# Packed attention and two MLP blocks on one core: the attention and weight steps of the next batch set beside other units

## The chip, the core and the metric

One core of a Trainium2 chip runs the whole program in one launch. The metric is device time in microseconds, the median of several runs. Three runs of the kernel before took 1697.84, 1701.42 and 1705.88 us, so runs of one kernel lie up to 0.5% apart.

## What is computed

Three stages in a row, all in float32 results:

```python
# 8 batches, 8 heads, 576 tokens, head size 64; 32 packed queries
p_packed = sm_attn(p, k, v)                  # 32 x 576 scores per head
out      = sm_attn(q, p_packed, p_packed)    # 576 x 32 scores per head
x = out.transpose(0, 2, 1, 3).reshape(4608, 512)
x = moe(x)    # h = x @ w_in (512 x 2048); (h * sigmoid(1.702 h)) @ w_out
y = moe2(x)   # g = x @ w_gate (512 x 1536); (silu(g) * (x @ w_val)) @ w_out2
```

The weights come as 64-bit floats and are turned into 32-bit ones on the chip. A float32 product is made as three products of a high and a low part (`split` makes the two parts, `mm3` issues the three matmuls).

## The kernel before

**Units.** The first MLP runs as 256 units: 8 batches, 2 halves of 288 tokens, 16 slices of 128 hidden columns. Unit n issues `u_p1(n)` (6 matmuls into a PSUM tile `h`), `act2` of unit n-1 (a copy on ScalarE, a subtraction on VectorE), `u_act1(n)` (tanh on ScalarE, a product `g` on VectorE, which frees `h`; there are two `h` tiles) and `p2` of unit n-3 (12 matmuls into the accumulators `acc`). A batch is 32 units, numbered u = 0 to 31 below. The second MLP follows after the last unit and is not touched.

**Steps beside the units.** While batch b goes through its units, the attention of batch b+1 is computed in small steps, and the weights of the second MLP are converted, six tiles of 128x512 in each of six batches. Which steps follow which unit is written out in two tables of text: `SECOND` has the steps of batch 1's attention beside the units n = 19 to 33 (the last 13 units of batch 0, and units 0 and 1 of batch 1), `STEADY` has those beside u = 0 to 31 of batches 1 to 6. Batch 0 and the first steps of batch 1's attention are in a third table, `FIRST`, and batch 7 has code of its own. The main loop issues the unit, then SECOND's steps, then STEADY's:

```python
        p2(units[n - LAG])
        if n in SECOND:
            issue(SECOND[n], ops, second)
        if 0 < b < B - 1 and u in STEADY:
            issue(STEADY[u], ops)
```

The program is laid out by a scheduler that takes this order as the order of preference: an instruction whose buffer is not yet free, or whose input is not ready by the scheduler's own reckoning, is put behind later ones of its engine. Once laid out, each engine, and SyncE as the queue that issues nearly all DMAs, goes through its instructions strictly in order.

**The steps, in the order in which a batch needs them** (g is one of two groups of four heads, j one of four raw tiles: K of g = 0, 1, then Q of g = 0, 1; e one of two halves):

- `raw_ahead n` loads a raw tile three ahead (four DMAs of 144 KB; three `raw` buffers, so each waits until `do_T` has read the tile that had the buffer); `v_ahead g` and `p_ahead` load V (five DMAs) and p of the batch after.
- `do_p`, `split_p`; `do_T j e` transposes a raw tile on VectorE (`T`, two buffers); `split_T j e` splits it (`Th`, two buffers), by ScalarE and GpSimd, or with `dve` by ScalarE and VectorE.
- `sc1 g` (12 matmuls), `max1`, `exp1`, `norm1`, `a1T` (5 transposes on TensorE), `copy_a1T`, `pv g` (20 matmuls): the first attention. `do_D g` copies its result out of PSUM in eight 32x32 copies on VectorE, or with `act` on ScalarE, and makes one masked copy on VectorE; `split_D`, `split_E` split both.
- `sc2 g t` (6 matmuls for one half t of the tokens), `max2`, `exp2`, `norm2` (five instructions on VectorE), `split_a2`: the second attention; the result `a2` is the moving operand of the next batch's `p1`.
- `win j` loads one of 16 tiles of the split `w_in` (512 KB) into a `wh` buffer, of which there are three. `do_z n` (n = 0 to 7) needs tiles 2n and 2n+1: four matmuls into two PSUM tiles `zp`, then copies, sums and a split on ScalarE, VectorE and GpSimd give `z`, the stationary operand of `p1`.
- `w2_stage i` loads a 64-bit weight tile into one of the same three `wh` buffers, `w2_rebias` and `w2_to_f32` convert it on ScalarE and VectorE, `w2_store` writes it back to DRAM.

All PSUM results of the attention (`sc`, `a1T`, `pv`, `zp`) share two buffers of one pool.

Of the kernel before, what the change touches and what calls it, by code (L numbers as in the profile page):

```python
# [53 lines left out]
"""  # L54

SECOND = {
# [15 lines left out]
}  # L72

STEADY = {
    0: "do_p; w2_stage 0",
    1: "split_p; p_ahead; do_T 0 0",
# [30 lines left out]
}  # L107


# [861 lines left out]
```

## Time and profile before

| | |
|---|---|
| time, median of 3 runs | 1701.42 us (1697.84 to 1705.88) |
| the profiled execution, time | 1701.6 us |
| its span | 1699.9 us |
| TensorE busy | 1633.9 us, 96% of the span |
| VectorE / ScalarE / GpSimd busy | 1208.0 (71%) / 773.8 (46%) / 291.6 us (17%) |
| mean granted TensorE clock | 0.994 of full speed |

Times inside the profile count from the start of the span, of which 1.7 us of the execution's own time lies outside. "PE" is TensorE, "DVE" VectorE, "ACT" ScalarE, "POOL" GpSimd, "SP" SyncE. A line such as L508 is a line of the kernel; L209 and L210 are the copy and the subtraction inside `split`, L220 the matmul inside `mm3`, L281 the DMA of `win`, L252 and L255 those of `load_raw` for K and Q, L339 the transpose of `do_T`, L508 and L511 the matmul and the sum of `do_z`, L558 the product of `u_act1`. In brackets stands the idle time of the engine before an instruction and what ended it.

### The profile page before, as it was taken

The page shows a single profiled execution, that of the slowest core. Times are in us where ns is not written, and L with a number is a line of the kernel's source. Part 1 is how long each engine was busy: PE and PEld are TensorE (multiplying, and loading weights), DVE is VectorE, ACT ScalarE, POOL GpSimd, SP SyncE. Part 2 cuts the span into 40 slices and gives each one's busy share as a digit, 9 for nine tenths or more (in the row PEclk, how much of TensorE's full clock was granted, in tenths as well). Part 3 has the DMA queues.
Part 4 walks back from the last instruction along what each step waited for, and adds up shares of the span by engine and source line. Part 5 has one row for each costly group of instructions (what it writes and reads, how often), then busy time and mean ns, then how long its engine had stood idle before and what let it go on. Part 6 is the DMA issues. An engine that isn't in the chain of part 4 may idle for free.

```text
span 1699.9 us, 25897 instructions
## 1 busy us (share of the span) xinstructions
PE 1633.9 (96%) x9264; PEld 1455.7 (86%) x9264; DVE 1208.0 (71%) x2284; ACT 773.8 (46%) x1606; POOL 291.6 (17%) x241
## 2 busy tenths in 40 slices
PE   5689999999999999999999999999999999999998
PEld 4569899999989999999988888888888888888887
DVE  6988988788777878868589366575567456756662
ACT  4775756657565665746455222242224222322222
POOL 1332403122121312202012110100010010001010
PEclk9989999999999999999999999999999999999999
DMA  8874856647364564616388554444444354425411
GB/s 232 297 240 108 255 163 209 199 161 240 119 203 143 202 206 142 225 41 221 109 288 324 206 178 153 149 130 155 143 160 155 95 175 163 149 77 171 151 50 50
DMA packets 169345, 290.60 MB, mean 171 GB/s; under 512 B 54784, under 2 KB 96768, under 8 KB 169216
## 3 DMA queue, kind: packets, MB, share of 16 engines
q1 hardware_dynamic: 165760, 280.03, 50.4%
q10 hardware_dynamic: 3456, 8.91, 1.5%
q8 instruction: 73, 1.20, 0.3%
q14 instruction: 56, 0.46, 0.1%
HBM read 230.16 MB, written 58.72 MB: 170 GB/s over the span
## 4 chain that ended last, share of the span: by engine, by line
PE 81%; DVE 8%; issue 4%; DMA 3%; ACT 2%; POOL 1%; SPq 0%; ACTq 0%; DVEq 0%; POOLq 0%
PE acc L220 34%; PE gv L220 29%; PE h L220 9%; PE sc L220 3%; PE pv L404 3%; PE zp L508 2%; DVE z L511 1%; DMA wh<-win 1%; DVE gh L210 1%; DVE g L558 1%; DVE f L205 1%; PE a1T L387 1%; DVE wc L203 0%; ACT z L510 0%; DMA w64in<-in_moe_w_in_dram 0%
## 5 line engine op out<-in xcount | busy, mean ns | idle before, releaser
L220 PE MATMUL gv<-xh,w 128*128 128x512 f32 x2304 | 554.4, 389 | 0.0
L220 PEld LDWEIGHTS gv<-xh,w 128*128 128x128 f32 x2304 | 432.4, 188 | 89.7
L220 PE MATMUL acc<-gh,wo 128*128 128x288 f32 x3072 | 457.8, 297 | 5.9 <-ACT wo L209 2.0
L220 PEld LDWEIGHTS acc<-gh,wo 128*128 128x128 f32 x3072 | 427.4, 190 | 10.3 <-ACT wo L209 2.9
L220 PE MATMUL acc<-wo,gh 128*128 128x512 f32 x1296 | 326.8, 389 | 0.4
L220 PEld LDWEIGHTS acc<-wo,gh 128*128 128x128 f32 x1296 | 243.0, 188 | 52.1 <-DVE c L214 1.7
L220 PE MATMUL h<-a,z 128*128 128x288 f32 x1536 | 253.6, 299 | 7.6 <-DVE g L558 6.0
L210 DVE TENSOR_TENSOR gh<-g,gh 128x288 fp32r<-128x288 f32 (+1 forms) x295 | 180.7, 612 | 89.1 <-ACT gh L209 87.3
L220 PEld LDWEIGHTS h<-a,z 128*128 128x128 f32 x1536 | 223.6, 191 | 18.0 <-DVE g L558 9.3
L209 ACT CAST gh<-g 128x288 fp32r<-128x288 f32 (+1 forms) x304 | 140.3, 461 | 176.9 <-DVE g L558 128.7
L210 POOL TENSOR_TENSOR gh<-s,gh 128x512 fp32r<-128x512 f32 x60 | 82.2, 1370 | 699.2 <-ACT gh L209 655.4
L802 DVE TENSOR_TENSOR c<-gv,c 128x512 f32<-128x512 f32 x192 | 132.1, 688 | 83.9 <-ACT tb L817 56.7
L209 ACT CAST gh<-s 128x512 fp32r<-128x512 f32 x60 | 37.3, 621 | 247.3 <-DVE s L813 229.5
L556 ACT ACTIVATE sig<-h 128x288 f32<-128x288 f32 x256 | 104.1, 408 | 86.9 <-PE h L220 82.5
L558 DVE SCALAR_TENSOR_TENSOR g<-sig,h 128x288 f32<-128x288 f32 x256 | 113.7, 444 | 33.7 <-ACT sig L556 30.9
L802 DVE TENSOR_TENSOR ta<-gv,c 128x512 f32<-128x512 f32 x96 | 66.1, 689 | 83.4 <-PE gv L220 83.4
L513 POOL TENSOR_TENSOR z<-z,z 128x512 fp32r<-128x512 f32 x56 | 75.0, 1339 | 170.9 <-ACT z L512 170.9
L511 DVE TENSOR_TENSOR z<-zp,z 64x512 f32<-64x512 f32 x112 | 77.0, 687 | 18.4 <-ACT z L510 15.3
L508 PE MATMUL zp<-wh,E 128*128 128x512 f32 x224 | 66.3, 404 | 12.6 <-DMA wh<-win 6.6
L822 ACT ACTIVATE s<-c 128x512 f32<-128x512 f32 x48 | 30.3, 632 | 95.9 <-DVE c L802 95.9
L510 ACT COPY z<-zp 64x512 f32<-64x512 f32 x112 | 65.0, 581 | 9.5 <-PE zp L508 7.0
L210 POOL TENSOR_TENSOR Th<-T,Th 128x576 fp32r<-128x576 f32 x30 | 44.2, 1483 | 125.2 <-ACT Th L209 125.2
(130 smaller groups left out, 1585.6 us busy)
## 6 DMA issues: line engine op xcount, KB each, us to landing
w<-w2s SPq DMA_DIRECT2D x144, 512.0 KB, 3.3
wh<-win SPq DMA_DIRECT2D x112, 512.0 KB, 4.2
w2s<-w SPq DMA_DIRECT2D x36, 512.0 KB, 3.8
w<-w2s SPq DMA_DIRECT2D x48, 256.0 KB, 2.6
raw<-in_k_dram SPq DMA_DIRECT2D x64, 144.0 KB, 3.9
raw<-in_q_dram SPq DMA_DIRECT2D x64, 144.0 KB, 4.0
x2d<-x SPq DMA_DIRECT2D x16, 576.0 KB, 3.8
w2d<-f SPq DMA_DIRECT2D x36, 256.0 KB, 3.2
```

The source lines that it names most:

```text
L209: ACT.copy(dst[:, 0], src)
L210: eng.tensor_tensor(out=dst[:, 1], in0=src, in1=dst[:, 0].bitcast(F32), op=ALU.subtract)
L220: PE.matmul(o, lhsT=lhs(a), rhs=rhs(c), start=first and n == 0, stop=last and n == 2)
L404: PE.matmul(ps[:, c].rearrange("p h i -> p (h i)"), lhsT=vv[:n, k, 2 * c:2 * c + 2].rearrange("p h d -> p (h d)"), rhs=st["a1T", g][:n, k, ...
L508: PE.matmul(ps, lhsT=E[:, c].rearrange("p a i -> p (a i)"), rhs=w[c][:, d], start=d == 0, stop=d == 1)
L510: ACT.copy(x[o], ps[r])
L511: DVE.tensor_tensor(out=x[o], in0=ps[o], in1=x[o], op=ALU.add)
L513: POOL.tensor_tensor(out=y[:, 1], in0=x, in1=y[:, 0].bitcast(F32), op=ALU.subtract)
L556: ACT.activation(s, ps[:, :HS], AF.Tanh, scale=0.5 * 1.702)
L558: DVE.scalar_tensor_tensor(out=g, in0=s, scalar=1.0, in1=ps[:, :HS], op0=ALU.add, op1=ALU.mult)
L802: DVE.tensor_tensor(out=o, in0=ps, in1=c, op=ALU.add)
L822: ACT.activation(s2, c2, AF.Tanh, scale=0.5)
```

## The change

Both tables are written anew. `FIRST`, the functions and the main loop stay as they are. The two tables hold the same steps as before, 71 and 113 of them, with these exceptions in their arguments: in `STEADY` `do_D 0` has `act`, `split_T 2 1` has `dve` and `split_T 3 1` has lost it; in `SECOND` `do_D 0` has `act` and `split_D 0` has `dve`. Everything else is a step at another unit, or at another place among the steps of its unit.

```diff
--- before.py
+++ after.py
@@ -54,56 +54,55 @@
 """
 
 SECOND = {
-    19: "+do_T 2 0; +max1 1; +exp1 1; +do_T 2 1; +win 0; +win 1; +win 2; +norm1 1",
-    20: "+a1T 0; +copy_a1T 0; +split_T 2 0 dve; +split_T 2 1; +raw_ahead 2",
-    21: "+pv 0; +do_D 0; +split_D 0; +split_E 0; +v_ahead 0; +a1T 1",
-    22: "+copy_a1T 1",
-    23: "+sc2 0 0; +max2 0 0; +pv 1; +do_D 1",
-    24: "+split_D 1; +split_E 1; +sc2 0 1; +max2 0 1; +do_T 3 0",
-    25: "+split_T 3 0 dve; +do_T 3 1; +do_z 0; +win 3; +win 4; +split_T 3 1 dve",
-    26: "+sc2 1 0; +raw_ahead 3; +max2 1 0; +do_z 1; +win 5; +win 6",
-    27: "+sc2 1 1; +v_ahead 1; +max2 1 1; +exp2 0 0; +do_z 2; +win 7; +win 8",
-    28: "+norm2 0 0; +exp2 1 0; +split_a2 0 0; +norm2 1 0; +exp2 0 1",
-    29: "+do_z 3; +win 9; +win 10; +split_a2 1 0; +norm2 0 1; +exp2 1 1",
-    30: "+split_a2 0 1; +norm2 1 1; +do_z 4; +win 11; +win 12; +split_a2 1 1",
-    31: "+do_z 5; +win 13; +win 14",
-    32: "+do_z 6; +win 15",
+    19: "+do_T 2 0; +split_T 2 0 dve; +win 1; +max1 1; +exp1 1; +win 4; +norm1 1; +raw_ahead 2; +do_T 2 1",
+    20: "+do_T 3 0; +win 0; +win 2; +a1T 0; +split_T 2 1",
+    21: "+copy_a1T 0; +pv 0; +win 3; +do_D 0 act; +split_D 0 dve; +raw_ahead 3",
+    22: "+a1T 1; +copy_a1T 1; +split_E 0; +do_T 3 1; +v_ahead 1",
+    23: "+sc2 0 0; +max2 0 0; +split_T 3 1 dve; +do_z 0; +pv 1; +do_D 1",
+    24: "+split_D 1; +split_E 1; +sc2 0 1; +exp2 0 0",
+    25: "+split_T 3 0 dve; +v_ahead 0",
+    26: "+sc2 1 0; +sc2 1 1; +do_z 1; +max2 0 1; +win 5; +win 6; +max2 1 0",
+    27: "+do_z 2; +win 7; +max2 1 1",
+    28: "+norm2 0 0; +win 8; +exp2 1 0; +split_a2 0 0; +norm2 1 0; +exp2 0 1; +win 13",
+    29: "+do_z 3; +split_a2 1 0; +norm2 0 1; +exp2 1 1; +win 9",
+    30: "+split_a2 0 1; +win 10; +norm2 1 1; +split_a2 1 1; +do_z 4; +win 11; +win 12",
+    31: "+do_z 5; +win 14",
+    32: "+win 15; +do_z 6",
     33: "+do_z 7",
 }
 
 STEADY = {
-    0: "do_p; w2_stage 0",
-    1: "split_p; p_ahead; do_T 0 0",
-    2: "w2_stage 1; do_T 0 1",
-    3: "w2_rebias 0; split_T 0 0; do_T 1 0; w2_to_f32 0",
-    4: "w2_stage 2; w2_store 0; split_T 0 1 dve; sc1 0; do_T 1 1",
-    5: "w2_rebias 1; max1 0; raw_ahead 0; w2_to_f32 1",
-    6: "exp1 0; w2_stage 3; w2_store 1; split_T 1 1; norm1 0",
-    7: "split_T 1 0; w2_rebias 2; w2_to_f32 2",
-    8: "raw_ahead 1; w2_stage 4; sc1 1; w2_store 2",
-    9: "do_T 2 0; w2_rebias 3; max1 1; exp1 1; w2_to_f32 3",
-    10: "do_T 2 1; w2_stage 5; w2_store 3; norm1 1; a1T 0",
-    11: "copy_a1T 0; pv 0; w2_rebias 4; split_T 2 1; raw_ahead 2; w2_to_f32 4",
-    12: "split_T 2 0 dve; w2_store 4; v_ahead 0; do_D 0",
-    13: "w2_rebias 5; split_D 0; split_E 0; a1T 1; w2_to_f32 5",
-    14: "copy_a1T 1; win 0; win 1; win 2; w2_store 5",
-    15: "pv 1; sc2 0 0",
-    16: "max2 0 0; do_D 1",
-    17: "split_D 1; split_E 1; sc2 0 1",
-    18: "v_ahead 1; max2 0 1; do_T 3 0; win 4; win 3",
-    19: "do_T 3 1; split_T 3 0 dve",
-    20: "do_z 0; split_T 3 1 dve; win 5; win 6",
-    21: "raw_ahead 3; sc2 1 0; max2 1 0; sc2 1 1",
-    22: "exp2 0 0; do_z 1; max2 1 1; win 7; win 8",
-    23: "exp2 1 0; norm2 0 0",
-    24: "exp2 0 1; do_z 2; norm2 1 0; split_a2 1 0; win 10; split_a2 0 0",
-    25: "exp2 1 1; win 9; norm2 0 1",
-    26: "do_z 3; win 11; win 12; win 14; split_a2 0 1; norm2 1 1",
-    27: "split_a2 1 1",
-    28: "win 13; do_z 4",
-    29: "win 15",
+    0: "w2_stage 0; do_T 0 0; do_p",
+    1: "split_p; w2_rebias 0; do_T 1 0",
+    2: "split_T 0 0; p_ahead",
+    3: "do_T 0 1; w2_to_f32 0",
+    4: "w2_store 0; split_T 0 1 dve; sc1 0; w2_stage 1; split_T 1 0",
+    5: "w2_rebias 1; w2_stage 4; do_T 1 1; w2_stage 2; max1 0; w2_to_f32 1",
+    6: "exp1 0; split_T 1 1",
+    7: "sc1 1; w2_rebias 2; w2_to_f32 2; w2_stage 3",
+    8: "max1 1",
+    9: "do_T 2 0; w2_rebias 3; w2_to_f32 3; norm1 0",
+    10: "w2_store 2; raw_ahead 1; split_T 2 0 dve; w2_store 1; a1T 0; do_T 2 1; w2_rebias 4",
+    11: "exp1 1; copy_a1T 0; norm1 1; w2_to_f32 4; pv 0; raw_ahead 2",
+    12: "w2_stage 5; do_D 0 act; w2_store 4; raw_ahead 0; a1T 1",
+    13: "copy_a1T 1; w2_rebias 5; split_E 0; do_T 3 0; split_D 0",
+    14: "w2_store 3; win 2",
+    15: "pv 1; split_T 2 1 dve; w2_to_f32 5; win 0; sc2 0 0",
+    16: "max2 0 0; do_D 1; v_ahead 0; split_T 3 0 dve",
+    17: "sc2 0 1; w2_store 5; win 1; v_ahead 1",
+    18: "split_E 1; exp2 0 0",
+    19: "do_T 3 1; win 3; win 7; split_T 3 1; max2 0 1",
+    20: "exp2 0 1; win 4; do_z 0; split_D 1; win 5",
+    21: "sc2 1 1; sc2 1 0; max2 1 0",
+    22: "win 6; exp2 1 0; max2 1 1; do_z 1; exp2 1 1",
+    23: "win 8; win 11; norm2 0 0",
+    24: "norm2 1 0; do_z 2; win 9; norm2 0 1; win 10; split_a2 1 0",
+    25: "raw_ahead 3",
+    26: "do_z 3; split_a2 0 1; win 12; split_a2 0 0",
+    27: "norm2 1 1; split_a2 1 1",
+    28: "do_z 4; win 13; win 14",
     30: "do_z 5",
-    31: "do_z 6; do_z 7",
+    31: "do_z 6; win 15; do_z 7",
 }
 
 
```

## Rows read from the trace of the kernel before

**Rows 1.** The page: busy time by engine; the clock in 40 slices.

```profile
PE 1633.9 (96%) x9264; PEld 1455.7 (86%) x9264; DVE 1208.0 (71%) x2284; ACT 773.8 (46%) x1606; POOL 291.6 (17%) x241
...
PEclk9989999999999999999999999999999999999999
```

**Rows 2.** Windows: bounds, length, busy per engine, granted clock, DMA share, GB/s.

```profile
141.10:190.80 49.70, 48.32 (x340) 45.63 (x339) 43.33 (x109) 29.23 (x68) 13.34 (x12) 1.00 0.61 178
190.80:291.40 100.60, 99.08 (x711) 95.68 (x710) 85.68 (x185) 61.73 (x142) 26.08 (x21) 1.00 0.65 202
...
691.20:790.10 98.90, 97.70 (x707) 94.95 (x706) 79.23 (x172) 58.04 (x134) 20.23 (x17) 1.00 0.42 145
```

**Rows 3.** Waits of PE, batches 1 to 6: total us, times, longest.

```profile
PE zp L508 <- DMA wh<-win: 6.6, 4, 2.9
PE zp L508 <- DVE z L511: 3.6, 6, 0.9
PE h L220 <- DVE g L558: 1.6, 1, 1.6
```

**Rows 4.** Waits of PE, SECOND's units of batch 0.

```profile
PE zp L508 <- DVE x L456: 0.7, 2, 0.6
PE zp L508 <- DVE z L511: 0.4, 1, 0.4
```

**Rows 5.** Waits of PE, the first 10 us of batch 7.

```profile
PE zp L508 <- DVE z L511: 1.1, 2, 0.7
```

**Rows 6.** Timeline of PE around do_z 4 of batch 2.

```profile
379.60 0.63 PE L508 MATMUL zp<-wh,E 128*128 128x512 f32 x2
381.92 0.70 PE L508 MATMUL zp<-wh,E 128*128 128x512 f32 x2 [1.69 <-DMA wh<-win]
```

**Rows 7.** Timeline of SP, its DMA issues, around do_z 1 to 4 of batch 2.

```profile
363.10 0.82 SPq L281 DMA_DIRECT2D wh<-win  x2
...
376.28 0.34 SPq L252 DMA_DIRECT2D raw<-in_k_dram  x1
376.73 0.87 SPq L281 DMA_DIRECT2D wh<-win  x2
```

**Rows 8.** Timeline of all engines before do_z 4 of batch 2.

```profile
373.53 1.65 POOL L513 TENSOR_TENSOR z<-z,z 128x512 fp32r<-128x512 f32 x1 [0.22 <-ACT z L512]
...
373.88 1.09 PE L508 MATMUL zp<-wh,E 128*128 128x512 f32 x4
...
373.94 1.55 DVE L210 TENSOR_TENSOR gh<-g,gh 128x288 fp32r<-128x288 f32 x1
...
375.54 0.71 DVE L339 STREAM_TRANSPOSE T<-raw 128x576 f32<-128x576 f32 x1
```

**Rows 9.** Timeline of SP around do_z 3 of batch 1.

```profile
275.67 0.80 SPq L281 DMA_DIRECT2D wh<-win  x2
```

**Rows 10.** Timeline of PE: do_z 3 of batch 1.

```profile
275.02 1.09 PE L508 MATMUL zp<-wh,E 128*128 128x512 f32 x4
```

**Rows 11.** Timeline of PE: do_z 1 and 2 of batch 2.

```profile
362.44 1.10 PE L508 MATMUL zp<-wh,E 128*128 128x512 f32 x4
...
368.16 1.09 PE L508 MATMUL zp<-wh,E 128*128 128x512 f32 x4
```

**Rows 12.** The two window loads issued at 363.10: landing times.

```profile
DMA to landing us min/median/max: 3.2/3.9/4.6
```

**Rows 13.** Timeline of all engines at units 5 and 6 of batch 4.

```profile
506.70 0.45 DVE L210 TENSOR_TENSOR gh<-g,gh 128x288 fp32r<-128x288 f32 x1
...
511.79 0.78 DVE L339 STREAM_TRANSPOSE T<-raw 128x576 f32<-128x576 f32 x1 [0.47 <-POOL Th L210]
...
512.96 0.80 PE L220 MATMUL h<-a,z 128*128 128x288 f32 x4 [1.57 <-DVE g L558]
```

**Rows 14.** Groups by line and form, 170 to 850 us: busy us, mean ns.

```profile
L416 DVE COPY dz<-pv 32x32 f32<-32x32 f32 x96 | 18.0, 187 | 25.2 <-PE pv L404 23.8
```

**Rows 15.** The copies of do_D on ACT, which the first batch uses.

```profile
L416 ACT COPY dz<-pv x8: 172/176/179, 41.0 to 42.3; 32x32 f32<-32x32 f32 x8
```

## The prediction

> **What bounds the kernel now.** I read the page first: TensorE is busy for 1633.9 of 1699.9 us and its clock is at the upper of its two levels (2.4 GHz) from the fourth slice on [rows 1]. Such a kernel can only gain where TensorE stands still, so the second view is that of windows. The first 141.1 us are FIRST's and the last 900 us the second MLP's; the change reaches neither. In the stretch that it does reach, TensorE is idle for 1.4 us (49.70 - 48.32) beside SECOND, 1.5 us in batch 1 and 1.2 us in batch 6, with VectorE busy for 80 to 85% of a batch and the granted clock at 1.00 throughout [rows 2]. A stall is therefore priced at its idle time alone: none there has brought the clock down.
>
> The third view, who waited for whom, names these stalls: in batches 1 to 6 TensorE waits 6.6 us for loads of `win`, 3.6 us for VectorE's sum in `do_z`, 1.6 us for the product that frees `h` [rows 3]; beside SECOND 0.7 + 0.4 us, all at `do_z` [rows 4]; and 1.1 us at the start of batch 7, for the last `do_z` of batch 6 [rows 5]. The sum, 6.6 + 3.6 + 1.6 + 0.7 + 0.4 + 1.1 = 14.0 us, is 0.8% of the span and about the most that an order of steps can win. A change of 0.5%, 8.5 us, is about the least that runs of this kernel tell from none; to be faster by that the new order must remove six tenths of all stalls. The loss has no such ceiling: a stall that it adds to a batch comes back up to six times.
>
> **The largest stall, and what makes it.** In batch 2 the second half of `do_z 4` (u = 28) waits 1.69 us [rows 6]. It needs window 9, whose buffer `do_z 3` frees. `do_z 3` starts at 373.88 [rows 8], but the two window loads go out at 376.73, 2.85 us later, because SP's queue holds a load of K for a later batch ahead of them, issued at 376.28 [rows 7], right after the transpose that frees its buffer ended (375.54 + 0.71 = 376.25) [rows 8]. That transpose belongs to the next batch's `do_T 1 1`, written at u = 4 and run a third of a batch ahead. In batch 1, where no load stands there, the windows go out at 275.67 for a `do_z 3` at 275.02, 0.65 us later [rows 9, 10]. So the stall is a blocked queue: it costs 1.7 to 2.9 us in a batch where it occurs, and nothing where it doesn't. The table's order is one of preference, and loads and transposes run far ahead of their units; so a move within the table only changes which of two ready instructions goes first.
>
> **The change, part by part.**
>
> *Transposes, norms and the load in the queue.* Next batch's `do_T 1 1` goes from u = 4 to 5 and its load, `raw_ahead 1` (four DMAs on SP), from u = 8 to 10; in this batch `norm2 0 1` goes from u = 25 to 24 and `norm2 1 1` from 26 to 27, so VectorE has nothing but the unit's own work at u = 25, ahead of `do_z 3`: room for that transpose before the windows' buffers come free. Bounds: 6.6 us gained (the queue is free each time, as in batch 1), or nothing. I take two thirds, 4.4 us, since the room is where it was missing; against it stands that window 9 is still behind another load of its pair (11 instead of 10).
>
> *Order of windows.* Each `do_z` frees two buffers. Before, the pairs loaded after `do_z 0` to `do_z 6` were (4,3), (5,6), (7,8), (10,9), (11,12), (14,13), (15); now (3,7), (4,5), (6,8), (11,9), (10,12), (13,14), (15). `do_z 1` and `do_z 6` now find their missing window first of its pair, and `do_z 2` must wait for both of a pair, the second included. The row nearest to it: pair (5,6) went out at 363.10 [rows 7], and the slower of the two landed 4.6 us after its issue [rows 12], at about 363.10 + 0.41 + 4.6 = 368.1; `do_z 2` began at 368.16 and reaches its second half about 0.5 us later [rows 11]. The margin is half a microsecond: free if the queue is, up to 1.69 us (the row of u = 28) in each of six batches, 10.1 us, if not. I take 0.25 us a batch, 1.5 us lost. Beside SECOND the windows come as 1, 4, 0, then 2, 3; 5, 6; 7, 8; 13, 9; 10, 11: `do_z 5` (n = 31) needs both 10 and 11, one unit after `do_z 4` freed them: by the 5.72 us from `do_z 1` to `do_z 2` two units later [rows 11] that is (5.72 - 1.09) / 2 + 1.09 = 3.4 us, less than the 4.6 us of a second load. Bounds: nothing (the scheduler puts units in between) and 1.69 us; I take 1.0 us lost.
>
> *`do_D 0` on ScalarE.* Eight copies of 187 ns leave VectorE [rows 14], 1.5 us a batch, and eight of 176 ns come to ScalarE [rows 15], 1.4 us. No wait of TensorE in batches 1 to 6 is for that step [rows 3], so nothing is gained there directly: 20 matmuls of `pv` and the next units cover it; without that cover it would be the 1.5 us. Beside SECOND it comes with `do_z 0` at n = 23 instead of 25, away from the transposes of `max2` for which `zp` waits. Bounds 0 and 1.1 us [rows 4]; I take 0.7 us gained, since the larger of the two waits there is for `max2`.
>
> *The stall on `h`.* It occurs once: in batch 4 the second of two transposes waits 0.47 us for GpSimd's split (its `T` buffer) with the product `g` queued behind it, and `p1` is 1.57 us late [rows 13]. `split_T 1 0` now precedes `split_T 1 1`, and `norm1 0` has left u = 6 for 9. Bounds 1.6 us and 0; half, 0.8 us gained.
>
> *The rest* I cost at nothing. The weight steps change units by one to four: 18 loads and 6 stores a batch on SP, 12 conversions on ScalarE and 12 on VectorE, for which TensorE never waits [rows 3]. They hold the `wh` buffers until `w2_to_f32 5`, now u = 15 instead of 13, still five units ahead of `do_z 0`; were that cover gone, the first window would cost a load's 3.2 to 4.6 us [rows 12]. `raw_ahead 0` (u = 5 to 12), `raw_ahead 3` (21 to 25, four loads of Q next to the windows of `do_z 3`), `v_ahead 0` and `1` (five loads each) move past windows in SP's order of preference; what they can do is stand ahead of a window: that is the loss in the rivals. Only `raw_ahead 0` now has its reader close by, `do_T 3 0` at u = 13; but its buffer is free from `do_T 0 1` (u = 3) on, so it can go out long before its unit, and if it doesn't, the eight units from u = 13 to `sc2 1` at u = 21 cover a late transpose. The chain of `do_z 5`, `6`, `7` at u = 30 and 31 keeps its units, so its 3.6 + 1.1 us stay.
>
> Sum: -4.4 + 1.5 + 1.0 - 0.7 - 0.8 = -3.4 us on the profiled execution's 1701.6 us, which is 0.2 us above the median: 1698.2, and 1698.0 us for the median.
>
> **The rivals.**
>
> 1. *The queue and the chain both come free* (faster). The 6.6 us go whole, the 1.6 us of `h` too, and half of the 4.7 us of the `do_z` chain, because window 13 now comes first: 10.6 us, about 1691. For it: batch 1 shows a `do_z 4` without a wait at the same two units' distance. Against: nothing moves `do_z 5` to `7`.
>
> 2. *Windows 4 and 5* (slower). The load that stood ahead of window 9 stands ahead of window 5, or `raw_ahead 3` at u = 25 does so for 9: `do_z 2` waits 1.69 us in each of six batches while nothing else is won, 10.1 us, about 1711.5; at the 2.9 us of the longest wait [rows 3] 17.4 us. It decides from a delay of the pair of 0.5 us on; batch 2's pair after `do_z 3` was delayed by 2.2 us (2.85 - 0.65). Against: between `do_z 1` and `do_z 2` the trace has no K load waiting in SP's queue [rows 7].
>
> 3. *GpSimd holds VectorE up* (slower). `split_T 3 1` now uses GpSimd at u = 19, next to `split_D 1` and the split of `do_z 0` at u = 20. With GpSimd in a split, `act2`'s subtraction on VectorE took 1.55 us [rows 8], and 0.45 us without [rows 13]. If that makes `h` late as in batch 4, 1.57 us in six batches is 9.4 us, about 1710.8. Against: `split_T 2 1` leaves GpSimd in turn, so the number of its splits is the same. The Trainium skill ("SBUF — State Buffer", "Who interferes with whom") says that a VectorE instruction with two SBUF inputs and a GpSimd instruction that reads SBUF share a read port, and that the later one blocks wholly; the two durations agree with it, and by it alone the place of each split, not their number, would make the time, which is this rival.
>
> 4. *Nothing moves*: what runs ahead does so whatever its unit, and the schedule comes out with the same stalls elsewhere: 1701.
>
> **How the numbers follow.** My forecast 0.40, rival 1 0.32, rival 2 0.15, rival 3 0.05, rival 4 0.08. Faster by over 0.5% (below 1692.9) is rival 1: 0.32. Slower (above 1709.9) is rivals 2 and 3: 0.20. Within 0.5%: 0.48. The likeliest case alone reaches from 1694 (all bounds of the gains: 6.6 + 1.1 + 1.6 = 9.3 less some new stall) to 1703 (none of the gains, half of 1.5 + 1.0 lost). The range for 8 in 10 takes in most of rival 1 and the lower half of rival 2: 1687 to 1712.
>
> **What would show it.** Right: the wait of `zp` for `win` at u = 28 of batches 2 to 4 is smaller or gone, with no K load ahead of its windows in SP's queue; a small wait appears at `do_z 2` (u = 24) and at n = 31; the 32x32 copies are half on ScalarE; the wait of `zp` for `do_z`'s sum stays near 4.7 us; batches are 98.5 to 100 us long. Wrong: a wait of over 1 us in every batch at a step that had none, above all at `do_z 2` or at a `p1` after u = 19; a batch of under 98.5 us with the `do_z` chain's wait gone; or a new wait at `sc1`, `a1T` or `pv`, which all had none and share two buffers with `zp`: `exp1 1` is now written behind `a1T 0`, which needs the buffers that it reads.

## The result, and the profile after

The change made the kernel faster by 0.84%: 1686.5 us (median of 6 runs, 1685.93 to 1687.7) against 1700.86 us (6 runs, 1697.84 to 1705.88) for the kernel before, ratio 0.9916, 95% interval 0.99 to 0.9932. The runs also lie closer together than before: 1.8 us apart instead of 8. The profiled execution's span is 1684.2 us, 15.7 us less.

Windows of the profile after, cut at the batches' first unit (columns as in [rows 2]): batches 1, 2, 4 and 6.

```profile
187.50:288.20 100.70, 99.55 (x717) 96.34 (x716) 82.92 (x182) 65.54 (x154) 26.75 (x23) 1.00 0.65 203
288.20:385.40 97.20, 97.01 (x707) 94.89 (x706) 77.49 (x170) 61.30 (x146) 22.82 (x19) 1.00 0.59 185
...
482.80:581.00 98.20, 97.68 (x708) 95.06 (x707) 76.68 (x171) 61.01 (x146) 23.07 (x19) 1.00 0.58 183
...
678.70:776.60 97.90, 97.35 (x708) 95.01 (x706) 74.26 (x164) 59.16 (x143) 19.53 (x17) 1.00 0.43 147
```

Batches 1 to 6 took 776.6 - 187.5 = 589.1 us, before 790.1 - 190.8 = 599.3 us [rows 2]: 10.2 us of the 15.7. TensorE's idle time in batch 6 fell from 1.20 to 0.55 us; in batch 2 it is 0.19 us. Of the rest, 909.8 - 907.6 = 2.2 us lie behind the first unit of batch 7 (the last `do_z` of batch 6, and batch 7's own units). The other 3.3 us lie ahead of batch 1. Of these, 1.2 us stand ahead of unit 19, at which the profile starts with 140.99 us (before 142.19); in the other programs of this study, all with the same `FIRST`, it starts between 140.03 (e16) and 143.23 (e6), in no order that follows their speed, so that part is no effect of the tables that these traces could tell from chance.

Waits of TensorE after, in three stretches: the end of batch 0, batches 1 to 6, the start of batch 7. They answer to [rows 3 to 5].

```profile
PE zp L507 <- DVE z L510: 0.2, 1, 0.2
...
PE zp L507 <- DVE z L510: 2.1, 4, 0.6
PE zp L507 <- DMA wh<-win: 0.7, 2, 0.5
...
PE zp L507 <- DVE z L510: 0.4, 1, 0.4
```

14.0 us of waits have become 3.4 us. Both large ones fell: that for window loads from 6.6 to 0.7 us, that for the sum of `do_z` from 3.6 + 0.4 + 1.1 = 5.1 to 2.7 us, and that of `p1` for the product is gone. So 10.6 of the 15.7 us between the two spans are waits of this list.

The blocked queue of batch 2, after. First SP's DMA issues, then the transpose and `do_z 2` among all engines' instructions, then TensorE at `do_z 3` and `do_z 4`.

```profile
364.30 0.34 SPq L251 DMA_DIRECT2D raw<-in_k_dram  x1
364.76 0.86 SPq L280 DMA_DIRECT2D wh<-win  x2
...
370.48 1.54 SPq L280 DMA_DIRECT2D wh<-win  x2
```

```profile
363.51 0.76 DVE L338 STREAM_TRANSPOSE T<-raw 128x576 f32<-128x576 f32 x1
364.10 1.10 PE L507 MATMUL zp<-wh,E 128*128 128x512 f32 x4
...
369.82 1.10 PE L507 MATMUL zp<-wh,E 128*128 128x512 f32 x4
...
375.54 0.64 PE L507 MATMUL zp<-wh,E 128*128 128x512 f32 x2
...
377.29 0.70 PE L507 MATMUL zp<-wh,E 128*128 128x512 f32 x2 [0.19 <-DMA wh<-win]
```

The next batch's transpose that frees a K buffer now ends at 364.27 (363.51 + 0.76), before the windows freed by `do_z 2` can go out, and the first of the four DMAs of the load of K goes out at 364.30, ahead of these windows. The windows behind `do_z 3` go out 0.66 us after it starts (370.48 - 369.82), as in batch 1 before [rows 9, 10], and no longer 2.85 us. The second half of `do_z 4` waits 0.19 us instead of 1.69 [rows 6]. It also stands elsewhere: a `p1` lies between the two halves now.

### The profile page after: what moved, and what is told of

Its sections match the earlier page's. It is cut to its first block, busy times and chain, and to the rows that moved or that the text cites. A ratio compares the mean times of both kernels' runs of the same rounds, so it can differ in the third digit from the quotient of the medians.

```text
span 1684.2 us, 25838 instructions
## 1 busy us (share of the span) xinstructions
PE 1630.0 (97%) x9264; PEld 1454.3 (86%) x9264; DVE 1182.5 (70%) x2229; ACT 781.9 (46%) x1662; POOL 292.9 (17%) x240
## 4 chain that ended last, share of the span: by engine, by line
PE 78%; DVE 12%; issue 5%; ACT 3%; DMA 2%; POOL 1%; SPq 0%; ACTq 0%; DVEq 0%; POOLq 0%
PE acc L219 32%; PE gv L219 29%; PE h L219 8%; PE sc L219 3%; PE pv L403 3%; DVE z L510 2%; DVE gh L209 2%; DVE g L557 1%; PE zp L507 1%; DVE f L204 1%; DVE wc L202 1%; DVE T L338 1%; PE a1T L386 1%; ACT z L509 1%; DVE x L471 1%
## 5 line engine op out<-in xcount | busy, mean ns | idle before, releaser
L209 DVE TENSOR_TENSOR gh<-g,gh 128x288 fp32r<-128x288 f32 (+1 forms) x295 | 175.6, 595 | 84.5 <-ACT gh L208 82.3
L805 ACT ACTIVATE s<-ta 128x512 f32<-128x512 f32 x48 | 30.3, 632 | 69.3 <-DVE ta L801 69.3
```

The source lines that it names most:

```text
L209: eng.tensor_tensor(out=dst[:, 1], in0=src, in1=dst[:, 0].bitcast(F32), op=ALU.subtract)
```

## The experiments

All ratios are to the kernel before on the same chip. Waits are those of TensorE between 138 and 790 us of each profile; the kernel before has there 6.6 us for windows and 4.0 us for the sum of `do_z`, the kernel after 0.7 and 2.7. (In the faster kernels this stretch takes in the start of batch 7, where the kernel before has 1.1 us more for the sum.)

**Which table.** e1 has the new `SECOND` with the old `STEADY`, e2 the reverse.

> Only the table SECOND is the new one. Adding up the two traces (units 19 to 31 of batch 0 took 48.6 us before and 46.5 us after; batch 1 took 100.6 and 100.7 us): 2 us faster than before, about 1699, ratio 0.9988, with batches 2 to 6 at 99 to 101 us and the wait of zp for win still at 6.6 us. If instead the order beside batch 0 shifts what runs ahead in later batches, the batches change too and the gain differs from 2 us by more than 2 us.

> Only the table STEADY is the new one. Adding up: 10 us in batches 1 to 6 and 2 us after them, about 1689, ratio 0.993; the waits of zp for win fall from 6.6 us to under 1 us and those for the sum of do_z from 4.7 us to about 2.5 us. If the gain were mostly SECOND's, ratio over 0.996.

e1: 1.0002 (0.999 to 1.0014), 1702.87 us. e2: 0.9921 (0.9907 to 0.9936), 1688.06 us. `STEADY` carries the gain. e2 has no wait for windows, as expected, but 4.2 us for the sum instead of the expected 2.5. In e1's profile the stretch from unit 19 to batch 1 did become shorter (141.90 to 188.8, 46.9 us, against 142.19 to 190.8, 48.6 us), but batch 1, with the old `STEADY`, took 102.4 instead of 100.6 us: given back in the next batch.

**The load of K in the queue.** e3 is the kernel before with six steps of `STEADY` moved; e4 is the kernel after with the same six put back.

```diff
-    0: "do_p; w2_stage 0",
-    1: "split_p; p_ahead; do_T 0 0",
-    2: "w2_stage 1; do_T 0 1",
-    3: "w2_rebias 0; split_T 0 0; do_T 1 0; w2_to_f32 0",
+    0: "do_p; do_T 0 0; w2_stage 0",
+    1: "split_p; p_ahead; do_T 1 0",
+    2: "w2_stage 1",
+    3: "w2_rebias 0; do_T 0 1; split_T 0 0; w2_to_f32 0",
...
-    5: "w2_rebias 1; max1 0; raw_ahead 0; w2_to_f32 1",
+    5: "w2_rebias 1; max1 0; do_T 1 1; w2_to_f32 1",
...
+    10: "do_T 2 1; raw_ahead 1; w2_stage 5; w2_store 3; norm1 1; a1T 0",
...
+    12: "split_T 2 0 dve; w2_store 4; v_ahead 0; raw_ahead 0; do_D 0",
...
```

> The kernel before with only do_T 0 and 1 (both halves) and raw_ahead 0 and 1 of STEADY at the new units. Theory 'queue' (the load of K stands ahead of window 9 in SyncE's queue because the transpose that frees its buffer comes after do_z 3): the transpose comes before do_z 2, the wait of zp for win falls from 6.6 us to 1 us or less, and the time by 5 to 6 us, ratio 0.9965. Rival 'rest' (the order of the windows, or the room that norm2 and do_D leave on VectorE): the wait stays at 5 us or more, ratio 1.000.

> The kernel after with the same six steps put back at the old units. Theory 'queue': the wait of zp for win is back at 4 to 6.6 us, about 1692, ratio to the kernel before 0.995. Rival 'rest': the wait stays under 1 us and the time at 1686.5, ratio 0.9915.

e3: 0.9964 (0.9952 to 0.9977), 1696.2 us. Its waits:

```profile
PE zp L508 <- DVE z L511: 6.5, 13, 0.9
...
PE zp L508 <- DVE g L558: 0.5, 1, 0.5
```

No wait for a window is left: the six steps alone empty the queue, worth 6 us. The waits for `do_z`'s sum even grew, so these have another cause. e4: 0.9923 (0.9908 to 0.9938), 1688.51 us, with 1.9 us of waits for windows: the wait came back, but not to 4 us as expected, and the time is not clearly above e2's or the change's. So in the old order the six steps are worth 6 us, and in the new one nothing that can be measured. Why is not shown. That the second half of `do_z 4` stands a `p1` later in the new order is not enough: it does so in e17 too (below), and waits there as long. The longest such wait of e4, in batch 3, and then that of e17 in batch 2:

```profile
478.88 0.70 PE L507 MATMUL zp<-wh,E 128*128 128x512 f32 x2 [1.70 <-DMA wh<-win]
```

```profile
380.65 0.70 PE L508 MATMUL zp<-wh,E 128*128 128x512 f32 x2 [2.02 <-DMA wh<-win]
```

**What makes the rest.** Each of the next five is the kernel after with one group of `STEADY`'s steps back at the old units (for e7, `do_D 0` without `act`); e9 and e10 divide the group of e6.

```diff
# e5: all 16 win, such as
-    19: "do_T 3 1; win 3; win 7; split_T 3 1; max2 0 1",
+    19: "do_T 3 1; split_T 3 1; max2 0 1",
...
# e9 (and, with e10's, e6)
-    24: "norm2 1 0; do_z 2; win 9; norm2 0 1; win 10; split_a2 1 0",
-    25: "raw_ahead 3",
-    26: "do_z 3; split_a2 0 1; win 12; split_a2 0 0",
-    27: "norm2 1 1; split_a2 1 1",
+    24: "do_z 2; norm2 1 0; win 9; split_a2 1 0; win 10; split_a2 0 0",
+    25: "raw_ahead 3; norm2 0 1",
+    26: "do_z 3; win 12; split_a2 0 1; norm2 1 1",
+    27: "split_a2 1 1",
# e10
...
-    21: "sc2 1 1; sc2 1 0; max2 1 0",
-    22: "win 6; exp2 1 0; max2 1 1; do_z 1; exp2 1 1",
+    21: "sc2 1 0; max2 1 0; sc2 1 1",
+    22: "exp2 0 0; win 6; max2 1 1; do_z 1",
...
```

> The kernel after with the 16 window loads of STEADY back at the old units. Theory 'windows' (what the transposes' order doesn't explain, some 5 us at the waits for do_z's sum, comes from the windows' new order): 1691, ratio 0.9942, waits of zp for the sum of do_z at 5 us or more (2.5 after). Rival 'not windows': 1687, ratio 0.992, those waits at 2 to 4 us.

> The kernel after with sc2, max2, exp2, norm2 and split_a2 of STEADY back at the old units. Theory 'last third' (these steps on VectorE, ScalarE and GpSimd around do_z 3 to 7 make the waits for do_z's sum): 1690 or more, ratio 0.9935, those waits at 5 us or more. Rival 'not these': 1687, ratio 0.992.

> The kernel after with do_D 0 of STEADY on VectorE again. By the prediction's step (no wait of TensorE is for it): 1686 to 1688, ratio 0.992. Rival (1.5 us of VectorE a batch are on the path): 1690 to 1695, ratio 0.995.

> The kernel after with norm2 and split_a2 of STEADY back at the old units (norm2 0 1 at 25, norm2 1 1 at 26, split_a2 0 0 at 24). Theory 'room' (VectorE and GpSimd must be empty between do_z 3 and do_z 7): 1694, ratio 0.995, the waits for do_z's sum at 5 us. Rival 'early exp2' (it is exp2, done up to four units sooner): 1688, ratio 0.992, the waits at 2 to 3 us.

> The kernel after with sc2, max2 and exp2 of STEADY back at the old units (exp2 0 0 at 22 instead of 18, exp2 0 1 at 24 instead of 20, exp2 1 1 at 25 instead of 22). Theory 'room': 1688, ratio 0.992. Rival 'early exp2' (norm2 and the splits of a2 wait for exp2, and pile up before do_z 5): 1694, ratio 0.995, the waits for do_z's sum at 5 us.

| run | ratio (interval) | waits: windows, `do_z`'s sum |
|---|---|---|
| e5, old windows | 0.9913 (0.9889 to 0.9936) | 1.2, 2.4 us |
| e6, old sc2, max2, exp2, norm2, split_a2 | 0.9949 (0.9933 to 0.9965) | 2.0, 5.6 us |
| e7, `do_D 0` on VectorE | 0.9915 (0.9888 to 0.9943) | 1.5, 2.0 us |
| e9, old norm2, split_a2 | 0.9911 (0.989 to 0.9932) | 1.0, 0.9 us |
| e10, old sc2, max2, exp2 | 0.9959 (0.9944 to 0.9973) | 1.5, 6.1 us |

The order of the windows, `do_D` on ScalarE and the moves of `norm2` and `split_a2` change nothing that can be measured. sc2, max2 and exp2 are worth some 7 us, and the waits for `do_z`'s sum follow them.

**Which of sc2, max2 and exp2.** e13 is the kernel before with these three kinds moved, e14 the same with e3's six steps; e15 is the kernel after with only exp2 put back; e17 and e18 touch a single line.

```diff
# e15, on the kernel after; the other three exp2 likewise
-    18: "split_E 1; exp2 0 0",
+    18: "split_E 1",
...
# e17, on the kernel before
-    21: "raw_ahead 3; sc2 1 0; max2 1 0; sc2 1 1",
+    21: "raw_ahead 3; sc2 1 1; sc2 1 0; max2 1 0",
# e18, on the kernel after
-    21: "sc2 1 1; sc2 1 0; max2 1 0",
+    21: "sc2 1 0; max2 1 0; sc2 1 1",
```

> The kernel before with only sc2, max2 and exp2 of STEADY at the new units (exp2 up to four units sooner, max2 0 1 one later). Theory 'early exp2 suffices': the waits for do_z's sum fall from 4.0 us to under 2.5 us, the waits for win stay at 5 us or more: 1698, ratio 0.9977. Rival 'only together with the other moves': ratio 1.000, both waits as before.

> The same, and the six steps do_T 0 and 1 and raw_ahead 0 and 1 moved as well. Theory (the two causes add: the queue and exp2): ratio 0.993, about 1690, waits for win under 1 us and for do_z's sum under 3 us. Rival 'only with the rest of STEADY': ratio 0.996, as with the six steps alone.

> The kernel after with only the four exp2 of STEADY back at the old units. Theory 'exp2' : ratio 0.996, 1694.5, as when sc2 and max2 went back with them. Rival 'max2 0 1 and the order of sc2 1 0 and 1 1': ratio 0.992.

> The kernel before with only unit 21 of STEADY rewritten: sc2 1 1 goes ahead of sc2 1 0 and of max2 1 0. Theory 'sc2' (with both products first, the second exp2 comes ready after ScalarE's copies of zp, not ahead of them): ratio 0.9955 as with sc2, max2 and exp2 moved together, waits for do_z's sum under 2.5 us. Rival 'all of them': ratio 0.998 to 1.000.

> The kernel after with only unit 21 of STEADY as before: sc2 1 0; max2 1 0; sc2 1 1. Theory 'sc2': 1694, ratio 0.9955, waits for do_z's sum at 5 us. Rival 'all of them': ratio 0.992 to 0.9935.

e13: 0.9955 (0.9935 to 0.9974). e15: 0.9918 (0.989 to 0.9945): exp2's units mean nothing: in batch 2 ScalarE starts each of the four within 0.01 us of where it does after, counted from the start of the unit that TensorE is at. In e13 the waits fell as expected (1.9 us for the sum, 5.2 for windows), the time by more. e17: 0.9947 (0.9931 to 0.9963), 1694.38 us; e18: 0.995 (0.9933 to 0.9968), 1693.66 us. One step moved ahead of two others of its unit (the swap, below) makes the old kernel faster by half a per cent, and its undoing takes some 0.3% from the new one. e14: 0.9921 (0.99 to 0.9943); the swap and the six steps multiply to 0.9947 x 0.9964 = 0.991. Put on the old kernel, these two are enough for the size of the whole change, as far as a product can say: no run has them alone, and e14 has e13's other moves too. They are not simply its two parts, for e4 keeps the change's time without the six steps. Waits of e17, e18 and e14:

```profile
PE zp L508 <- DMA wh<-win: 7.3, 4, 2.0
PE zp L508 <- DVE z L511: 2.0, 5, 0.5
```

```profile
PE zp L507 <- DVE z L510: 5.7, 9, 1.0
PE zp L507 <- DMA wh<-win: 2.6, 2, 1.5
```

```profile
PE zp L508 <- DVE z L511: 2.1, 6, 0.5
PE zp L508 <- DVE gh L210: 1.6, 1, 1.6
```

The first halves the waits for the sum and leaves those for windows; the second brings the former back; in e14 no wait for a window is left. But these waits are only part of what the swap wins. From the kernel before to e17 batches 1 to 6 became 4.0 us shorter, of which 3.1 us are idle time of TensorE, while the medians differ by 8.7 us; the rest shows in no wait of these two profiles, and its cause stays open.

**GpSimd's subtraction.** In e8 (on the kernel before) and e16 (on e10's) GpSimd writes zeros where `do_z` wants the low part of z, so the low part is left out. In e11 (on the kernel after) and e12 (on the kernel before) the subtraction of `do_z 4` to `7` is done on VectorE, with nothing left out.

```diff
-            POOL.tensor_tensor(out=y[:, 1], in0=x, in1=y[:, 0].bitcast(F32), op=ALU.subtract)
# e8, e16
+            POOL.memset(y[:, 1].bitcast(F32), 0.0)
# e11, e12
+            (DVE if n >= 4 else POOL).tensor_tensor(out=y[:, 1], in0=x, in1=y[:, 0].bitcast(F32), op=ALU.subtract)
```

> The kernel before, where GpSimd writes zeros in the low part of z of do_z from batch 1 on instead of the subtraction (so z has its high part only); GpSimd then reads nothing of SBUF there. Theory 'port' (act2's subtraction takes 1.3 instead of 0.45 us while GpSimd subtracts, and this delays the product, the copies of zp and do_z's sum): no such subtraction over 0.8 us around do_z 4 to 7, the waits for do_z's sum fall from 4.7 to under 2 us, those for win stay near 6.6 us; time 3 us shorter, 1698, ratio 0.998. Rival 'distance' (do_z 5, 6, 7 follow each other too closely): the waits stay near 4.7 us, ratio 1.000.

> The kernel after with sc2, max2 and exp2 at the old units, where in addition GpSimd writes zeros in the low part of z from batch 1 on instead of the subtraction (z has its high part only). Theory 'port' (late exp2 costs time because do_z's subtraction on GpSimd then falls on act2's one on VectorE): the waits for do_z's sum fall from 6.1 us to under 2 us, ratio 0.991. Rival 'order' (the waits come from the order of VectorE's and ScalarE's instructions alone): waits at 5 us or more, ratio 0.995.

> The kernel after, with the subtraction of do_z 4 to 7 (batches 1 to 7) on VectorE instead of GpSimd; nothing is left out. Theory 'port' (GpSimd's subtraction makes act2's one 0.85 us longer and so delays the copies of zp): the rest of the waits for do_z's sum (2.7 us) falls to 1 us, time 1684.5, ratio 0.9903. Rival 'load' (VectorE, 0.69 us more in each of four do_z): 1688 or more.

> The kernel before with the same edit. Theory 'port': the waits for do_z's sum fall from 4.0 us to under 2 us, those for win stay at about 6 us; 1698, ratio 0.998. If GpSimd's subtraction also makes the transpose ahead of the load of K late, the waits for win fall too, as with the zeros, and it comes to 1690. Rival 'load': ratio 1.000 or more.

e8: 0.9915 (0.9892 to 0.9939), far more than the 3 us expected: no wait for `do_z`'s sum, and only 2.3 us for windows. e16: 0.9896 (0.9873 to 0.9918), where the 6.1 us of e10 are gone. Groups by line of the kernel before and of e8 (190 to 780 us): `act2`'s subtraction.

```profile
L210 DVE TENSOR_TENSOR gh<-g,gh 128x288 fp32r<-128x288 f32 x189 | 117.7, 623 | 39.9 <-ACT gh L209 38.5
```

```profile
L210 DVE TENSOR_TENSOR gh<-g,gh 128x288 fp32r<-128x288 f32 x193 | 90.0, 466 | 43.1 <-ACT gh L209 41.8
```

With GpSimd reading nothing there, the same instruction takes 466 ns in the mean instead of 623. So with the old order at u = 21, in e8 and e16, the waits for the sum hang on GpSimd's subtraction: on what it does to VectorE's, on its own length (1347 ns in the mean before, 527 ns for the zeros), or on both. e11: 0.991 (0.9893 to 0.9926), no better than the change, and its waits for the sum stay at 2.4 us where 1 was expected; e12: 0.9985 (0.9968 to 1.0003), not clear of no change. In e12 the waits for the sum fall from 4.0 to 1.4 us, but those for windows stay at 5.9 us, and one of 2.4 us for the product comes new: nearly what was won for the sum. No version here that leaves nothing out is clearly faster than the change.

## Why the prediction was wrong

The direction of the sum was right (-3.4 us), its size was not: 14.4 us, and the time lies 0.5 us below the range. The chances gave 0.32 to what happened, rival 1, and even that at 1691 us. Its reason for the chain, that window 13 now comes first, was not what did it: e5 has the old order of windows and the time of the change.

**The step that failed** is "The chain of `do_z 5`, `6`, `7` at u = 30 and 31 keeps its units, so its 3.6 + 1.1 us stay". The units stayed, and about half of these waits went, 4.7 to 2.1 + 0.4 = 2.5 us. What the step lacked is the one line at u = 21: `sc2 1 1` ahead of `sc2 1 0` and `max2 1 0`. The prediction costed it nowhere; both steps keep their unit. e17 (1703.1 - 1694.38 = 8.7 us) and e18 (1693.66 against 0.9916 x 1703.1 = 1688.8, 4.9 us) put 5 to 9 us on it. What it does can be read behind `do_z 1` of batch 2. In the kernel before, whose `zp` matmuls start at 362.44 [rows 11], the timeline of all engines goes on:

```profile
363.49 0.45 ACT L464 ACTIVATE x<-x 128x288 f32<-128x288 f32 x1
...
363.96 1.19 ACT L510 COPY z<-zp 64x512 f32<-64x512 f32 x2
...
364.11 0.80 DVE L469 TENSOR_REDUCE sm<-x 128x9 f32<-128x288 f32 x2
...
364.83 1.40 DVE L511 TENSOR_TENSOR z<-zp,z 64x512 f32<-64x512 f32 x2
```

and in e17:

```profile
359.89 1.15 PE L508 MATMUL zp<-wh,E 128*128 128x512 f32 x4
...
360.55 1.19 ACT L510 COPY z<-zp 64x512 f32<-64x512 f32 x2 [0.24 <-PE zp L508]
...
361.24 1.37 DVE L511 TENSOR_TENSOR z<-zp,z 64x512 f32<-64x512 f32 x2
361.77 0.44 ACT L464 ACTIVATE x<-x 128x288 f32<-128x288 f32 x1
```

Before, the second `exp2` and VectorE's first sums of `norm2` stand ahead of `do_z`'s copies and sum, which start 1.52 and 2.39 us after the matmuls. With the swap the second `exp2` stands behind the copies, and they start after 0.66 and 1.35 us: `do_z 1`'s sum starts a microsecond sooner behind its matmuls, and what follows shifts. It is so in batches 1, 2, 3 and 5 alike: the second `exp2` starts 0.12 us into unit 23 before and 0.11 us in e18, but 0.89 to 0.95 us in e17 and after. At the other end, `do_z 5` and `6` of batch 5 in the kernel before:

```profile
686.80 1.29 POOL L513 TENSOR_TENSOR z<-z,z 128x512 fp32r<-128x512 f32 x1 [3.92 <-ACT z L512]
...
687.09 1.32 DVE L210 TENSOR_TENSOR gh<-g,gh 128x288 fp32r<-128x288 f32 x1 [0.53 <-ACT gh L209]
...
688.34 0.44 DVE L558 SCALAR_TENSOR_TENSOR g<-sig,h 128x288 f32<-128x288 f32 x1
...
689.88 1.41 DVE L511 TENSOR_TENSOR z<-zp,z 64x512 f32<-64x512 f32 x2 [0.15 <-ACT z L510]
...
690.62 0.73 PE L508 MATMUL zp<-wh,E 128*128 128x512 f32 x2 [0.87 <-DVE z L511]
```

and after:

```profile
675.05 1.30 POOL L512 TENSOR_TENSOR z<-z,z 128x512 fp32r<-128x512 f32 x1 [3.31 <-ACT z L511]
675.32 0.46 DVE L557 SCALAR_TENSOR_TENSOR g<-sig,h 128x288 f32<-128x288 f32 x1 [0.51 <-ACT sig L555]
...
676.27 0.46 DVE L209 TENSOR_TENSOR gh<-g,gh 128x288 fp32r<-128x288 f32 x1 [0.50 <-ACT gh L208]
...
676.88 1.41 DVE L510 TENSOR_TENSOR z<-zp,z 64x512 f32<-64x512 f32 x2
...
678.20 0.63 PE L507 MATMUL zp<-wh,E 128*128 128x512 f32 x2
```

Before, `act2`'s subtraction starts behind GpSimd's and takes 1.32 us; the product, ScalarE's copies and the sum of `do_z 5` queue behind it, and `do_z 6` waits 0.87 us. After, the product comes first and the subtraction starts as GpSimd ends: 0.46 us, and no wait. e8 and e16, in which GpSimd reads nothing at this step, have no such waits, though there the step itself is shorter too. Such meetings did not become fewer: over batches 1 to 6 `act2`'s subtraction takes 607 ns in the mean after, 603 in e17 and 606 in e18 (623 before). If they make the difference, it is by where they fall. How the swap at u = 21 leads, link by link, to another place of GpSimd's subtraction at u = 30 is not shown, and stays open.

**The other terms.** The queue: 4.4 us taken, e3 measures 6; the mechanism was right, but its cause was put on room for VectorE at u = 25 (`norm2`), which e9 shows to be worth nothing. It is the order of the four transposes and two loads. Windows 4 and 5 both behind `do_z 1` (+1.5 us): no wait at `do_z 2` in any batch. `SECOND`'s windows (+1.0) and its earlier `do_z 0` (-0.7): e1 has 0, within 2 us; the profile after has no wait for a window at n = 31, and one of 0.5 us at `do_z 6`, in batch 1. So the second step that failed is the 2.5 us of losses: with the queue, 1.9 us were to be won at the windows, and 5.9 us of their waits went. `do_D 0` on ScalarE: nothing, as said. The stall on `h` (-0.8): gone, 1.6 us. Rival 2 (a load ahead of window 5) didn't occur. Rival 3 had a mechanism that the runs show, a GpSimd subtraction holding up VectorE, but at `split_T` and as a loss; where it shows in TensorE's waits, it is `do_z`'s split, and these waits became smaller.

**The ceiling.** The list of waits, 14.0 us, was taken as about the most to be won; 14.4 us were won with 3.4 us of waits left. Of batch 7 it took only the first 10 us; behind them the profile before has a wait for the product (below) that the profile after lacks. So of the 15.7 us between the two profiles 10.6 are waits of the list, 1.1 this wait, and 1.2 lie ahead of unit 19; the other 2.8 us are in none of these. In batches 1 to 6 the length fell by 10.2 us and TensorE's idle time by some 9 us (from 599.3 - 587.3 = 12.0 to 589.1 - 586.1 = 3.0 us, length less busy time summed over the six windows of each profile). The list is also of one execution, while the times of the kernel before scatter by 8 us.

```profile
PE h L220 <- DVE g L558: 1.1, 2, 0.7
```

## What to carry to other kernels

Where a list scheduler lays out the program, compare the order inside a unit as closely as the units: here one step moved ahead of two others of its unit was worth about as much (5 to 9 us) as the six moves that emptied the queue (6 us). The waits here that stood in some batches only, at `do_z 4`, `6` and `7`, came and went with moves made elsewhere in the table; price such a wait at its full size on the gain side, and do not take the list of waits as a ceiling. Do not add gains that were measured apart: the six moves were worth 6 us in the old order and nothing that can be measured in the new one. Before naming what frees a queue, look which instruction stands at its head and what that one waits for.

## What the runs showed of the hardware

A VectorE subtraction of two SBUF tiles (128x288) took 0.46 us alone and 1.32 us when it started 0.29 us behind a GpSimd subtraction of 1.29 us, that is, it ended 0.32 us after that one. Of `act2`'s 189 between 190 and 780 us of the kernel before, 52 start while GpSimd runs an instruction that reads SBUF; each ends 0.31 us or more after that one, and they take 1084 ns in the mean, the other 137 only 448 ns. With GpSimd only writing at `do_z` (e8), the mean of all was 466 ns. The Trainium skill ("SBUF — State Buffer", "Who interferes with whom") says that a VectorE instruction with two SBUF inputs contends with a GpSimd instruction that reads SBUF, and not with one that only writes it; these runs agree.

What the runs add is how much can hang on it: 157 ns more in the mean for one instruction of VectorE, which is busy for 80% of a batch, goes with some 13 us of a program that TensorE bounds (1701.8 - 1688.52 us in e8). Not all of that need be the collision: the zeros also make GpSimd's own step of `do_z` shorter, 527 instead of 1347 ns in the mean, and these runs don't separate the two.
